# A WaveNet convolution kernel: a prologue with another load order, halo zeros set ahead, early staging copies on ScalarE and no filler matmuls

## The chip, the cores and the metric

The kernel runs on one core of one Trainium2 chip. The time is the device time of one execution in microseconds (us). Most executions of one kernel agree within about 0.3%. Before the change the median of the first three runs was 325.55 us (324.85 to 325.66).

## The reference

Sixteen thousand time steps of 144 channels in two batches go through a causal convolution of 15 taps at distance 2, a gate, and an output projection. All tensors are bf16.

```python
# x (2, 16000, 144), w (15, 144, 288), w_o (144, 144)
dil = 2
pad = (K - 1) * dil                       # 28 steps of halo
xp = jnp.pad(x, ((0, 0), (pad, 0), (0, 0)))
h = sum(einsum('btc,cd->btd', xp[:, pad - i*dil : pad - i*dil + T, :], w[i]) for i in range(K))
f, g = h[..., :D], h[..., D:]
z = jnp.tanh(f) * sigmoid(g)
return z @ w_o
```

## The kernel before

The 128 SBUF partitions hold 2 batches x 64 segments of 250 time steps. A partition also needs the 28 steps before its segment (its halo). For partitions 0 and 64, which start a batch, this halo is zero. The 144 channels are split into 128 ("A") and 16 ("B"). Names that the profile uses:

- `Xp` is the prologue's input (38 steps, loaded in four pieces), `Xr` the ring of later input chunks of 16 steps. `WA` are the 15 taps of the 128 channels, loaded in four pieces, youngest taps last. `WB` holds the weights of the 16 channels. `WOR` holds the output weights, 16 small loads on GpSimd's queue.
- `XA` and `XB` hold the input transposed. In the prologue TensorE transposes it (`ID,Xp`), and VectorE or ScalarE evacuates the bank (copies the result from `PS`, where TensorE writes, to SBUF). `UX` is a matmul result that ScalarE evacuates for a later addition on VectorE. Later input is copied to the staging buffers `STA` and `STB`, and a DMA transposes from there. `XBc` is a compacted copy of the 16 channels.
- The first ten steps are convolved directly (`WA,XA` and `WB,XB` matmuls). After them a fast scheme works on differences of inputs (`V`, `DU`, `DD`, `GU`, `GV`, `GX`, `GD`) and sums of weights (`WC`, `WS`, `WT`, `WV`, `WD`), both made on VectorE.

A small list scheduler in the kernel orders each engine's instructions at build time from estimated durations. An added or moved instruction can therefore reorder many others. The prologue's loads and fillers:

```python
wa_pieces = [(0, 4), (4, 8), (8, 12), (12, 15)]
pro_pieces = [(0, 14), (14, 22), (22, E0), (E0, EP)]
n16 = ((NP - 1) // 16) * 16                        # 112
for pi, (e0, e1) in enumerate(pro_pieces):
    if pi:
        ...  # g.add("sp", ld_w(t0, t1), ...): w3, w2, w1 ahead of x1, x2, x3
    if e0 >= H:
        ...  # last piece: all 128 partitions in one load
        continue
    g.add("sp", ld_x(flat(Xp[1:1 + n16, e0:e1, :]), 1, 1 + n16, e0, e1), ...)      # 112 partitions
    g.add("sp", ld_x(flat(Xp[1 + n16:NP, e0:e1, :]), 1 + n16, NP, e0, e1), ...)    # 15 partitions
...  # partition 0: two loads on ScalarE's queue
wa_op = g.add("sp", ld_w(t0, t1), w=[("WA", 0)], ...)       # w0, the youngest taps
...
warm(40)                                   # 40 matmuls that nobody reads, while the first load is under way
for pi in range(4):
    ...                                    # transposes, evacuation, compaction of piece pi
    warm(WARMS)                            # 8 filler matmuls
for o in range(-4, 0):
    ...                                    # VectorE memsets of the halo columns of XA
...                                        # GpSimd: zf, zf, fix: halo zeros of XBc
```

The staging copies, and what waits for the last weights:

```python
def load_xa(o):
    ...
    g.add("dve", lambda v: v.tensor_copy(STA[:, q, :, :], Xr[:, ci % NX, i0:i0 + 8, 0:DA]), ...)
    g.add("sp", lambda e: e.dma_start_transpose(XA[:, s, :, :], ...STA...), ...)
...
load_xchunk(0).deps.add(wa_op)             # input chunk 0 is issued when w0 has landed
...
op = g.add("pool", f, r=["WORz"], w=[("WORp", dl, part)], dma="wor", ...)   # output weights
op.deps.add(wa_op)
```

Of the kernel before, what the change touches and what calls it, by code (L numbers as in the profile page):

```python
# [327 lines left out]
def _conv_wavenet_kernel(nc, x, w, w_o, out):  # L328
# [39 lines left out]
    WARMS = 8  # L368
    LAG = 2
    PATTERNS = {29: 'O2 O1 Y01 Y0a D11 O0 Y0b D01 D00 D10', 28: 'Y0a X0a+ O1+ Y0b X0b+ O2+ D11 S0+ D10 X1a+ D00 Y01 S1+ X1b+ VE+ O0+ D01 VF+', 1: 'Y0a O2+ X0a+ Y0b X0b+ D11 X1a+ O1+ D00 S0+ D10 Y01 S1+ X1b+ D01 VE+ VF+ O0+', 0: 'Y0a X0a+ Y0b D11 X0b+ D00 X1a+ O2+ O1+ O0+ S0+ D10 Y01 S1+ X1b+ D01 VE+ VF+', 2: 'Y0a O2+ X0a+ O1+ Y0b X0b+ D11 D00 S0+ X1a+ D10 Y01 S1+ X1b+ D01 VE+ O0+ VF+'}  # L370
    SPREAD = 12
# [3 lines left out]
    with contextlib.ExitStack() as st:  # L375
# [111 lines left out]
        wa_pieces = [(0, 4), (4, 8), (8, 12), (12, 15)]  # L487
        pro_pieces = [(0, 14), (14, 22), (22, E0), (E0, EP)]
        n16 = ((NP - 1) // 16) * 16
        for pi, (e0, e1) in enumerate(pro_pieces):  # L490
            if pi:
                t0, t1 = wa_pieces[4 - pi]
                g.add("sp", ld_w(t0, t1), w=[("WA", 4 - pi)], dur=0.55, dma="wa", nbytes=(t1 - t0) * 128 * N2 * 2)
            if e0 >= H:
                g.add("sp", ld_x(flat(Xp[:, e0:e1, :]), 0, NP, e0, e1), w=[("Xp", pi, 0), ("Xp", pi, 1)], dur=0.45, dma="xp", nbytes=NP * (e1 - e0) * D * 2)
                continue
            g.add("sp", ld_x(flat(Xp[1:1 + n16, e0:e1, :]), 1, 1 + n16, e0, e1), w=[("Xp", pi, 0)], dur=0.45, dma="xp", nbytes=n16 * (e1 - e0) * D * 2)
            g.add("sp", ld_x(flat(Xp[1 + n16:NP, e0:e1, :]), 1 + n16, NP, e0, e1), w=[("Xp", pi, 1)], dur=0.45, dma="xp", nbytes=15 * (e1 - e0) * D * 2)
        g.add("act", lambda e: e.dma_start(flat(Xp[0:1, 0:H, :]), bass.AP(x_t, 0, [[L * D, 1], [1, H * D]])), w=[("Xp", 0, 2)], dur=0.5, dma="xp", nbytes=8064)
        g.add("act", lambda e: e.dma_start(flat(Xp[0:1, H:E0, :]), bass.AP(x_t, 0, [[L * D, 1], [1, KD * D]])), w=[("Xp", 2, 2)], dur=0.5, dma="xp", nbytes=576)  # L500
        t0, t1 = wa_pieces[0]
        wa_op = g.add("sp", ld_w(t0, t1), w=[("WA", 0)], dur=0.55, dma="wa", nbytes=(t1 - t0) * 128 * N2 * 2)
        xp_keys = [[("Xp", 0, 0), ("Xp", 0, 1), ("Xp", 0, 2)], [("Xp", 1, 0), ("Xp", 1, 1), ("Xp", 0, 2)],
                   [("Xp", 2, 0), ("Xp", 2, 1), ("Xp", 0, 2), ("Xp", 2, 2)], [("Xp", 3, 0)]]
# [11 lines left out]
        g.add("pool", lambda p: p.memset(Z[:], 0.0), w=[("Z", i) for i in range(NZ)], dur=1.2)  # L516
# [55 lines left out]
        for o in range(-4, 0):  # L572
            i0 = 2 if o == -4 else 0
            i1 = 6 if o == -1 else 8
            def zc(v, o_=o, i0_=i0, i1_=i1):
                dst = XA[:, aslot(o_), i0_:i1_, :].rearrange("p s (b q) -> p s b q", q=SEG)[:, :, :, 0]
                return v.memset(dst, 0.0)
            g.add("dve", zc, w=[("XA", aslot(o))], dur=0.08)
        hk = ["XBc_h%d" % i for i in range(4)]
        hk5 = hk + ["XBc_h4"]  # L580
        for b in range(B):
            def zf(p, b_=b):
                return p.memset(XBc[b_ * SEG:b_ * SEG + 1, 4:8, MB - H // 4 - 1:MB, :], 0.0)
            g.add("pool", zf, r=hk, w=hk + ["XBcz"], dur=0.35)


        def fix(p):
            s = Xp[:, H:E0, DA:D]
            dst = bass.AP(XBc[:].tensor, 6 * MB * DB + (MB - 1 - H // 4) * DB, [[8 * MB * DB, NP], [MB * DB, 2], [1, DB]])
            return p.tensor_copy(dst, s)  # L590
        g.add("pool", fix, r=xp_keys[2], w=hk, dur=0.3)
# [24 lines left out]
        def load_xchunk(ci):  # L616
            a, c = CH[ci]
            s = ci % NX
            return g.add("sp", ld_x(flat(Xr[:, s, 0:c - a, :]), 0, NP, E0 + a, E0 + c), w=[("Xr", s)], dur=0.5, dma="xr", nbytes=NP * (c - a) * D * 2)

        def compact_chunk(ci):
            a, c = CH[ci]
            s = ci % NX
            cmp_op("dve", Xr[:, s, 0:c - a, DA:D], E0 + a, E0 + c, [("Xr", s)], ("XBc", ci), 0.16 + (c - a) * DB / 1900.0)

        def diff_b(eng, m0, nm, r, tag):
# [5 lines left out]
            g.add(eng, f, r=r, w=[tag], dur=t_tt(4 * nm * DB), prio=2, soft=gate[:1])  # L632
# [5 lines left out]
        def load_xa(o):  # L638
# [3 lines left out]
            g.add("dve", lambda v: v.tensor_copy(STA[:, q, :, :], Xr[:, ci % NX, i0:i0 + 8, 0:DA]),  # L642
                  r=[("Xr", ci % NX)], w=[("STA", q)], dur=0.335, prio=2, soft=gate[:1])
# [3 lines left out]
        def load_xb(o, parts=(0, 1)):  # L647
# [10 lines left out]
            for h in parts:  # L658
                def cp(v, h=h):
                    src = bass.AP(XBc[:].tensor, (MB - 1 - m4 - h) * DB, [[8 * MB * DB, NP], [MB * DB, 6], [1, 128]])  # L660
                    return v.activation(STB[:, q, 6 * h:6 * h + 6, :], src, ACT.Copy)  # L661
                g.add("act", cp, r=sorted(ck, key=str), w=[("STB", q, h)], dur=0.708, prio=2, soft=gate[:1])
# [657 lines left out]
```

## Time and profile before

| | before |
|---|---|
| time, median of the first 3 runs | 325.55 us |
| span of the profiled run | 323.8 us |
| TensorE busy, 50 to 300 us | 249.98 of 250 us |
| first real work on TensorE | 5.62 us |
| first WB,XB / first WC,GX / first WA,GD / first projection | 21.53 / 31.09 / 40.87 / 46.82 us |

From the page of the kernel before, the head and the chain of work that ended last (shares of the span by engine):

```profile
span 323.8 us, 7023 instructions
...
PE 315.0 (97%) x2702; PEld 245.1 (76%) x2702; DVE 284.3 (88%) x616; ACT 265.3 (82%) x630; POOL 17.1 (5%) x29
...
## 4 chain that ended last, share of the span: by engine, by line
PE 89%; ACT 4%; DVE 3%; DMA 2%; issue 1%; POOL 0%; ACTq 0%; POOLq 0%
```

PE is TensorE's matmuls, PEld its weight loads. TensorE is the limit. VectorE (88%) is near, but has only 3% of the chain. Stretches of the same run, with columns: from and to, length, then busy time and instruction count of PE, PEld, DVE, ACT and POOL, then the granted clock, the share of time that the 16 DMA engines were busy, and GB/s. (The share sums the times of the packets, so it can pass 1: it is 1.35 from 20 to 25 us of this run.)

```profile
2.00:4.00 2.00, 2.00 (x21) 2.00 (x20) 0.00 (x0) 0.89 (x2) 2.00 (x1) 1.00 0.88 258
50.00:150.00 100.00, 99.98 (x841) 77.05 (x840) 94.31 (x201) 89.09 (x214) 0.00 (x0) 1.00 0.77 155
150.00:250.00 100.00, 100.00 (x846) 77.63 (x844) 94.18 (x200) 89.22 (x216) 0.00 (x0) 1.00 0.81 167
250.00:300.00 50.00, 50.00 (x422) 38.60 (x420) 41.40 (x85) 41.23 (x101) 0.00 (x0) 1.00 0.53 102
```

From 50 us on there is nothing to win by reordering: the sum of the last three PE columns is 249.98 us of 250. While the first inputs arrive, the DMA engines are 88% busy.

TensorE's weight-load timeline shows the prologue (start, duration, line, operands, how many; in brackets the idle time before it and what ended it):

```profile
5.62 0.82 PEld L559 LDWEIGHTS PS<-ID,Xp 128*128 128x128 bf16 x14
6.82 0.45 PEld L535 LDWEIGHTS PS<-ONES,ID 128*128 128x128 bf16 x8 [0.38 <-DVE XA L568]
...
21.53 1.45 PEld L729 LDWEIGHTS PS<-WB,XB 128*128 128x128 bf16 x12
...
26.42 0.11 PEld L729 LDWEIGHTS PS<-WT,DU 128*128 128x128 bf16 x2 [1.00 <-DVE DU L681]
...
30.79 0.24 PEld L729 LDWEIGHTS PS<-WA,XA 128*128 128x128 bf16 x3 [1.31 <-ACT UX L956]
...
40.87 0.11 PEld L729 LDWEIGHTS PS<-WA,GD 128*128 128x128 bf16 x2 [0.66 <-DVE PS L1020]
...
46.82 0.28 PEld L828 LDWEIGHTS PS<-WOR,ZT 128*128 128x128 bf16 x3
```

The second line is one of four filler groups (`ONES,ID`). The three large gaps sum to 2.97 us, and all begin after 25 us. The last line is the first projection. The chain of waits tells what they wait for (start, duration, what):

```profile
16.41 0.34 DVE STA L642
...
16.99 2.58 ACT STB L661 x4
19.56 6.65 DMA XB<-STB
...
26.24 1.58 ACT STB L661 x2
...
30.20 0.55 ACT UX L956
...
30.79 8.27 PE PS L729 x66
```

The staging copies for chunk 0 begin at 16.4 us, the first staged transpose takes 6.65 us from issue to landing, and ScalarE, held by its staging buffers, is late for the `UX` evacuation. That opens the gap of 1.31 us.

The load of chunk 0 was issued at 11.34 us, and the view of DMA issues (how many, KB, us from issue to landing) has for it:

```profile
Xr<-in_x_dram SPq DMA_DIRECT2D x1, 576.0 KB, 3.7
```

So it had landed at about 15.0 us, and VectorE, busy with weight sums, first read it at 16.20 us.

### The profile page before, as it was taken

Reading aid. Unit: us, or ns where it says so; the run is one execution under the profiler, and the core shown is the slowest. Engines: PE = TensorE matmul, PEld = TensorE weight load, DVE = VectorE, ACT = ScalarE, POOL = GpSimd, SP = SyncE. Lnnn points to the kernel's source line nnn. Section 1 sums busy time; section 2 is a strip of 40 time slices with the busy share of each in tenths; the row PEclk is TensorE's granted clock in tenths of the full one; section 3 lists DMA queues with packets and bytes.
Section 4 is the critical chain, followed back from the end, with each engine's and each line's share of the span. In section 5 each row is a group of like instructions: output and inputs, shape, how many; then the busy total and the mean of one; then the engine's idle time right before and its main releaser. Section 6 shows DMA issues by size and latency. Waiting matters only on the chain.

```text
span 323.8 us, 7023 instructions
## 1 busy us (share of the span) xinstructions
PE 315.0 (97%) x2702; PEld 245.1 (76%) x2702; DVE 284.3 (88%) x616; ACT 265.3 (82%) x630; POOL 17.1 (5%) x29
## 2 busy tenths in 40 slices
PE   7997999999999999999999999999999999999994
PEld 7875767777777777777777777777777777777774
DVE  1989979899898989989898998989899998884774
ACT  3666588979798998979898897989889797778674
POOL 8750000000000000000000000000000000000000
PEclk9999999999999999999999999999999999999999
DMA  8899992948849496897929888795958479161553
GB/s 210 277 119 224 188 236 63 183 134 159 220 92 222 102 201 169 126 238 106 249 69 218 154 167 189 90 225 122 224 141 175 102 115 197 37 75 75 109 125 97
DMA packets 127822, 50.40 MB, mean 156 GB/s; under 512 B 119134, under 2 KB 121615, under 8 KB 127789
## 3 DMA queue, kind: packets, MB, share of 16 engines
q1 hardware_dynamic: 127273, 49.62, 74.4%
q0 software_dynamic: 512, 0.33, 0.5%
q8 instruction: 21, 0.34, 0.4%
q14 instruction: 12, 0.10, 0.1%
q10 hardware_dynamic: 4, 0.01, 0.0%
HBM read 11.82 MB, written 9.22 MB: 65 GB/s over the span
## 4 chain that ended last, share of the span: by engine, by line
PE 89%; ACT 4%; DVE 3%; DMA 2%; issue 1%; POOL 0%; ACTq 0%; POOLq 0%
PE PS L729 77%; PE PS L828 9%; DMA XB<-STB 2%; ACT STB L661 2%; PE PS L535 1%; DVE WC L610 1%; ACT TS L750 1%; ACT TS L753 0%; ACT PS L887 0%; DVE V L681 0%; DVE WT L610 0%; DVE WD L610 0%; ACT XA L568 0%; PE PS L859 0%; PE PS L786 0%
## 5 line engine op out<-in xcount | busy, mean ns | idle before, releaser
L1008 DVE TENSOR_TENSOR Xp<-PS,UX 128x576 f32<-128x576 f32 x90 | 62.8, 750 | 20.4 <-PE PS L729 20.1
L729 PE MATMUL PS<-WB,XB 128*128 128x288 bf16 x260 | 71.9, 286 | 0.0
L729 PE MATMUL PS<-WA,GD 128*128 128x288 bf16 x360 | 69.9, 286 | 0.4 <-DVE PS L1020 0.4
L1020 DVE TENSOR_TENSOR PS<-PS,Xp 128x576 f32<-128x576 f32 x90 | 68.2, 758 | 2.1 <-ACT OS L836 1.0
L750 ACT ACTIVATE TS<-PS 128x288 f16<-128x288 f32 x125 | 51.6, 413 | 15.0 <-PE PS L729 14.0
L836 ACT ACTIVATE OS<-PS 128x432 bf16<-128x432 f32 (+1 forms) x88 | 42.3, 488 | 13.8 <-PE PS L828 12.8
L661 ACT ACTIVATE STB<-XBc 128x768 bf16<-128x768 bf16 x60 | 50.5, 849 | 3.4 <-DMA XB<-STB 2.0
L753 ACT ACTIVATE TS<-PS 128x288 f16<-128x288 f32 x125 | 51.4, 411 | 0.0
L887 ACT ACTIVATE PS<-PS 128x288 f32<-128x288 f32 x120 | 46.1, 405 | 4.2 <-PE PS L729 4.1
L956 ACT ACTIVATE UX<-PS 128x576 f32<-128x576 f32 x60 | 39.2, 654 | 10.4 <-PE PS L729 10.1
L729 PE MATMUL PS<-WS,GU 128*128 128x288 bf16 x210 | 44.3, 287 | 0.0
L828 PE MATMUL PS<-WOR,ZT 128*128 128x144 bf16 (+1 forms) x322 | 42.4, 253 | 0.0
L729 PEld LDWEIGHTS PS<-WA,GD 128*128 128x128 bf16 x360 | 34.6, 98 | 10.0 <-DVE PS L1020 1.2
L758 DVE TENSOR_TENSOR Z<-TS 128x288 bf16<-128x288 f16 x125 | 36.7, 298 | 4.5 <-ACT TS L753 4.2
L729 PE MATMUL PS<-WC,XB 128*128 128x288 bf16 x120 | 34.3, 286 | 0.0
L828 PEld LDWEIGHTS PS<-WOR,ZT 128*128 128x128 bf16 x322 | 27.9, 98 | 6.3 <-ACT OS L836 0.5
L729 PE MATMUL PS<-WD,DD 128*128 128x288 bf16 x180 | 31.9, 286 | 0.5 <-ACT PS L887 0.5
L729 PE MATMUL PS<-WC,V 128*128 128x288 bf16 x180 | 30.6, 286 | 0.0
L729 PE MATMUL PS<-WA,DD 128*128 128x288 bf16 x180 | 30.6, 286 | 0.0
L729 PEld LDWEIGHTS PS<-WB,XB 128*128 128x128 bf16 x260 | 25.4, 98 | 6.4
L729 PE MATMUL PS<-WT,DU 128*128 128x288 bf16 x120 | 24.5, 286 | 0.8 <-DVE DU L681 0.7
L729 PEld LDWEIGHTS PS<-WS,GU 128*128 128x128 bf16 x210 | 18.5, 98 | 7.5 <-ACT PS L887 0.3
(80 smaller groups left out, 468.7 us busy)
## 6 DMA issues: line engine op xcount, KB each, us to landing
Xr<-in_x_dram SPq DMA_DIRECT2D x15, 576.0 KB, 4.5
out_dram<-OS SPq DMA_DIRECT2D x30, 288.0 KB, 3.2
WA<-in_w_dram SPq DMA_DIRECT2D x3, 288.0 KB, 5.0
ZT<-Z SPq DMA_TRANSPOSE x32, 3.7
Xp<-in_x_dram SPq DMA_DIRECT2D x2, 252.0 KB, 4.8
XA<-STA SPq DMA_TRANSPOSE x30, 3.5
XB<-STB SPq DMA_TRANSPOSE x30, 4.8
Xp<-in_x_dram SPq DMA_DIRECT2D x1, 441.0 KB, 3.9
```

What stands on the lines that cost most here:

```text
L535: g.add("pe", [lambda t: t.matmul(PS[:, BANK_O * 512:BANK_O * 512 + 128], lhsT=ID[:], rhs=ONES[:], start=True, stop=True)] * n, r=["ID", " ...
L661: return v.activation(STB[:, q, 6 * h:6 * h + 6, :], src, ACT.Copy)
L729: return lambda t: t.matmul(bank(bk.b), lhsT=lhs(), rhs=rhs(), start=start, stop=True, skip_group_check=True)
L750: return a.activation(TS[:, s, 0, :, :], both(bk, 0, D), ACT.Tanh)
L753: return a.activation(TS[:, s, 1, :, :], both(bk, D, D), ACT.Sigmoid)
L758: return v.tensor_tensor(dst, TS[:, s, 0, :, :], TS[:, s, 1, :, :], ALU.mult)
L828: return t.matmul(PS[:, c0:c0 + n * D], lhsT=ZT[:, zt, blk, :], rhs=WOR[:, wi:wi + n, :].rearrange("p a b -> p (a b)"), start=first, stop= ...
L836: return e.tensor_copy(dst, src) if eng == "dve" else e.activation(dst, src, ACT.Copy)
L887: g.add("act", lambda e: e.activation(bank(bk.b + 1), bank(bk.b), ACT.Copy), w=[bk], dur=t_act(N2), prio=0)
L956: g.add("act", lambda e: e.activation(UX[:, k, u % NU, :, :], both(X, 0, N2), ACT.Copy), r=[X], w=[("UX", k, u % NU)], frees=[X], dur=t_ac ...
L1008: g.add("dve", lambda v, k=k, wi=wi, vb=vb, us=us: v.tensor_tensor(wslot(wi), both(vb, 0, N2), UX[:, k, us, :, :], ALU.add), r=[vb, ("UX", ...
L1020: return v.tensor_tensor(both(d, 0, N2), src, wslot(wi), ALU.add)
```

## The change

The intent is to have the staged transposes begin earlier: chunk 0 is loaded ahead of the youngest weights, its staging copies go to ScalarE, the halo zeros are written before any data lands, later loads keep out of the first transposes' way, and TensorE no longer runs fillers. The core of the diff:

```diff
-    WARMS = 8
+    WARMS = 0
...
+    EARLY = 4
+    EARLYC = 1
...
+        LOADS = [("x", 0), ("w", 3), ("w", 2), ("x", 1), ("w", 1), ("x", 2), ("x", 3), ("r", 0), ("w", 0)]
...
-            g.add("sp", ld_x(flat(Xp[1:1 + n16, e0:e1, :]), 1, 1 + n16, e0, e1), ...)
-            g.add("sp", ld_x(flat(Xp[1 + n16:NP, e0:e1, :]), 1 + n16, NP, e0, e1), ...)
+            for i, p0 in enumerate((0, SEG)):
+                g.add("sp", ld_x(flat(Xp[p0 + 1:p0 + SEG, e0:e1, :]), p0 + 1, p0 + SEG, e0, e1), ...)   # 63 partitions
...
+        for zi, (e0, e1) in enumerate(((0, 14), (14, H))):
+            for p0 in (0, SEG):
+                g.add("dve", lambda v, ...: v.memset(flat(Xp[p0:p0 + 1, e0:e1, :]), 0.0), ...)
...
-            g.add("dve", zc, w=[("XA", aslot(o))], dur=0.08)
...  (GpSimd's zf, zf and fix are gone too)
-            cmp_op("dve", Xr[:, s, 0:c - a, DA:D], ...)
+            cmp_op("act" if ci <= EARLYC else "dve", Xr[:, s, 0:c - a, DA:D], ...)
...
+            if o <= EARLY:
+                g.add("act", lambda a: a.activation(STA[:, q, :, :], src, ACT.Copy), ...)
+            else:
+                g.add("dve", lambda v: v.tensor_copy(STA[:, q, :, :], src), ...)
...
-        load_xchunk(0).deps.add(wa_op)
+        if ("r", 0) not in LOADS:
+            load_xchunk(0).deps.add(wa_op)
...
-                op.deps.add(wa_op)            # output weights
+                op.deps.add(xb2)              # xb2: the second staged transpose
...
-                load_xchunk(nl[0]).deps.add(wa_op)
+                load_xchunk(nl[0]).deps.add(wa_op if nl[0] < 2 else xb2)
```

The full diff also changes what the scheduler may do (priorities, work held back until the second staged transpose, the bank of one accumulator, finer tracking of `Z`).

More of the change, by code (lines that the diff above doesn't have):

```diff
@@ L487, in _conv_wavenet_kernel, with load_xchunk @@
         wa_pieces = [(0, 4), (4, 8), (8, 12), (12, 15)]
+        LOADS = [("x", 0), ("w", 3), ("w", 2), ("x", 1), ("w", 1), ("x", 2), ("x", 3), ("r", 0), ("w", 0)]
         pro_pieces = [(0, 14), (14, 22), (22, E0), (E0, EP)]
-        n16 = ((NP - 1) // 16) * 16
-        for pi, (e0, e1) in enumerate(pro_pieces):
-            if pi:
-                t0, t1 = wa_pieces[4 - pi]
-                g.add("sp", ld_w(t0, t1), w=[("WA", 4 - pi)], dur=0.55, dma="wa", nbytes=(t1 - t0) * 128 * N2 * 2)
+        def load_xchunk(ci):
+            a, c = CH[ci]
+            s = ci % NX
+            return g.add("sp", ld_x(flat(Xr[:, s, 0:c - a, :]), 0, NP, E0 + a, E0 + c), w=[("Xr", s)], dur=0.5, dma="xr", nbytes=NP * (c - a) * D * 2)
@@ L494, in _conv_wavenet_kernel @@
+        wa_ops = {}
+        for what, pi in LOADS:
+            if what == "w":
+                t0, t1 = wa_pieces[pi]
+                wa_ops[pi] = g.add("sp", ld_w(t0, t1), w=[("WA", pi)], dur=0.42, dma="wa", nbytes=(t1 - t0) * 128 * N2 * 2)
+                continue
+            if what == "r":
+                load_xchunk(pi)
+                continue
+            e0, e1 = pro_pieces[pi]
             if e0 >= H:
-                g.add("sp", ld_x(flat(Xp[:, e0:e1, :]), 0, NP, e0, e1), w=[("Xp", pi, 0), ("Xp", pi, 1)], dur=0.45, dma="xp", nbytes=NP * (e1 - e0) * D * 2)
+                g.add("sp", ld_x(flat(Xp[:, e0:e1, :]), 0, NP, e0, e1), w=[("Xp", pi, 0), ("Xp", pi, 1)], dur=0.48, dma="xp", nbytes=NP * (e1 - e0) * D * 2)
@@ L496, in _conv_wavenet_kernel @@
                 continue
-            g.add("sp", ld_x(flat(Xp[1:1 + n16, e0:e1, :]), 1, 1 + n16, e0, e1), w=[("Xp", pi, 0)], dur=0.45, dma="xp", nbytes=n16 * (e1 - e0) * D * 2)
-            g.add("sp", ld_x(flat(Xp[1 + n16:NP, e0:e1, :]), 1 + n16, NP, e0, e1), w=[("Xp", pi, 1)], dur=0.45, dma="xp", nbytes=15 * (e1 - e0) * D * 2)
-        g.add("act", lambda e: e.dma_start(flat(Xp[0:1, 0:H, :]), bass.AP(x_t, 0, [[L * D, 1], [1, H * D]])), w=[("Xp", 0, 2)], dur=0.5, dma="xp", nbytes=8064)
-        g.add("act", lambda e: e.dma_start(flat(Xp[0:1, H:E0, :]), bass.AP(x_t, 0, [[L * D, 1], [1, KD * D]])), w=[("Xp", 2, 2)], dur=0.5, dma="xp", nbytes=576)
@@ L501, in _conv_wavenet_kernel @@
-        t0, t1 = wa_pieces[0]
-        wa_op = g.add("sp", ld_w(t0, t1), w=[("WA", 0)], dur=0.55, dma="wa", nbytes=(t1 - t0) * 128 * N2 * 2)
-        xp_keys = [[("Xp", 0, 0), ("Xp", 0, 1), ("Xp", 0, 2)], [("Xp", 1, 0), ("Xp", 1, 1), ("Xp", 0, 2)],
-                   [("Xp", 2, 0), ("Xp", 2, 1), ("Xp", 0, 2), ("Xp", 2, 2)], [("Xp", 3, 0)]]
+            for i, p0 in enumerate((0, SEG)):
+                g.add("sp", ld_x(flat(Xp[p0 + 1:p0 + SEG, e0:e1, :]), p0 + 1, p0 + SEG, e0, e1), w=[("Xp", pi, i)], dur=0.48, dma="xp", nbytes=63 * (e1 - e0) * D * 2)
@@ new lines, in _conv_wavenet_kernel @@
+        for p0 in (0, SEG):
+            g.add("act", ld_x(flat(Xp[p0:p0 + 1, H:E0, :]), p0, p0 + 1, H, E0), w=[("Xp", 2, 2 + p0)], dur=0.5, dma="xp", nbytes=576)
+        for zi, (e0, e1) in enumerate(((0, 14), (14, H))):
+            for p0 in (0, SEG):
+                g.add("dve", lambda v, p0=p0, e0=e0, e1=e1: v.memset(flat(Xp[p0:p0 + 1, e0:e1, :]), 0.0), w=[("XpZ", zi, p0)], dur=1.1)
+        xpz = [[("XpZ", zi, p0) for p0 in (0, SEG)] for zi in range(2)]
+        xp_keys = [[("Xp", 0, 0), ("Xp", 0, 1)] + xpz[0], [("Xp", 1, 0), ("Xp", 1, 1)] + xpz[1],
+                   [("Xp", 2, 0), ("Xp", 2, 1), ("Xp", 2, 2), ("Xp", 2, 2 + SEG)] + xpz[1], [("Xp", 3, 0), ("Xp", 3, 1)]]
@@ L506, in ld_wb @@
+        wa_op = wa_ops[0]
         def ld_wb(par):
@@ L515, in _conv_wavenet_kernel @@
         g.add("pool", lambda p: p.memset(XBc[:, 4:6, MB - 1, :], 0.0), w=["XBcz"], dur=0.2)
-        g.add("pool", lambda p: p.memset(Z[:], 0.0), w=[("Z", i) for i in range(NZ)], dur=1.2)
+        g.add("pool", lambda p: p.memset(Z[:], 0.0), w=[("Z", i, d) for i in range(NZ) for d in range(8)], dur=1.2)
         g.add("pool", lambda p: p.memset(WOR[:], 0.0), w=["WORz"], dur=1.9)
@@ L571, in _conv_wavenet_kernel @@
             warm(WARMS)
-        for o in range(-4, 0):
-            i0 = 2 if o == -4 else 0
-            i1 = 6 if o == -1 else 8
-            def zc(v, o_=o, i0_=i0, i1_=i1):
-                dst = XA[:, aslot(o_), i0_:i1_, :].rearrange("p s (b q) -> p s b q", q=SEG)[:, :, :, 0]
-                return v.memset(dst, 0.0)
-            g.add("dve", zc, w=[("XA", aslot(o))], dur=0.08)
         hk = ["XBc_h%d" % i for i in range(4)]
         hk5 = hk + ["XBc_h4"]
-        for b in range(B):
-            def zf(p, b_=b):
-                return p.memset(XBc[b_ * SEG:b_ * SEG + 1, 4:8, MB - H // 4 - 1:MB, :], 0.0)
-            g.add("pool", zf, r=hk, w=hk + ["XBcz"], dur=0.35)
-        def fix(p):
-            s = Xp[:, H:E0, DA:D]
-            dst = bass.AP(XBc[:].tensor, 6 * MB * DB + (MB - 1 - H // 4) * DB, [[8 * MB * DB, NP], [MB * DB, 2], [1, DB]])
-            return p.tensor_copy(dst, s)
-        g.add("pool", fix, r=xp_keys[2], w=hk, dur=0.3)
         for o, tiles, bb in ((-1, range(E0 - 4, E0), 7), (0, range(E0, E0 + 8), 6)):
@@ L614, in chunk_of @@
             return [ci for ci, (a, c) in enumerate(CH) if a <= t < c][0]
-        def load_xchunk(ci):
-            a, c = CH[ci]
-            s = ci % NX
-            return g.add("sp", ld_x(flat(Xr[:, s, 0:c - a, :]), 0, NP, E0 + a, E0 + c), w=[("Xr", s)], dur=0.5, dma="xr", nbytes=NP * (c - a) * D * 2)
         def compact_chunk(ci):
@@ L623, in compact_chunk @@
             s = ci % NX
-            cmp_op("dve", Xr[:, s, 0:c - a, DA:D], E0 + a, E0 + c, [("Xr", s)], ("XBc", ci), 0.16 + (c - a) * DB / 1900.0)
+            cmp_op("act" if ci <= EARLYC else "dve", Xr[:, s, 0:c - a, DA:D], E0 + a, E0 + c, [("Xr", s)], ("XBc", ci), 0.16 + (c - a) * DB / 1900.0)
         def diff_b(eng, m0, nm, r, tag):
@@ L631, in f @@
                 return v.tensor_tensor(pat(2, -2 * MB * DB), pat(6, -2 * MB * DB), pat(4, 2 * MB * DB + DB), ALU.subtract)
-            g.add(eng, f, r=r, w=[tag], dur=t_tt(4 * nm * DB), prio=2, soft=gate[:1])
+            g.add(eng, f, r=r, w=[tag], dur=t_tt(4 * nm * DB), prio=2 if gate else 0, soft=gate[:1])
         def diff_chunk(ci):
@@ L641, in load_xa @@
             i0 = 8 * o - CH[ci][0]
-            g.add("dve", lambda v: v.tensor_copy(STA[:, q, :, :], Xr[:, ci % NX, i0:i0 + 8, 0:DA]),
-                  r=[("Xr", ci % NX)], w=[("STA", q)], dur=0.335, prio=2, soft=gate[:1])
+            src = Xr[:, ci % NX, i0:i0 + 8, 0:DA]
+            if o <= EARLY:
+                g.add("act", lambda a: a.activation(STA[:, q, :, :], src, ACT.Copy), r=[("Xr", ci % NX)], w=[("STA", q)], dur=0.92, prio=1, soft=gate[:1])
+            else:
+                g.add("dve", lambda v: v.tensor_copy(STA[:, q, :, :], src), r=[("Xr", ci % NX)], w=[("STA", q)], dur=0.335, prio=2, soft=gate[:1])
             g.add("sp", lambda e: e.dma_start_transpose(XA[:, s, :, :], STA[:, q, :, :].rearrange("p a b -> p (a b)")),
@@ L661, in cp @@
                     return v.activation(STB[:, q, 6 * h:6 * h + 6, :], src, ACT.Copy)
-                g.add("act", cp, r=sorted(ck, key=str), w=[("STB", q, h)], dur=0.708, prio=2, soft=gate[:1])
+                g.add("act", cp, r=sorted(ck, key=str), w=[("STB", q, h)], dur=0.708, prio=2 if gate else 0, soft=gate[:1])
             if 1 not in parts:
                 return
-            g.add("sp", lambda e: e.dma_start_transpose(XB[:, s, :, :], STB[:, q, :, :].rearrange("p a b -> p (a b)")),
+            return g.add("sp", lambda e: e.dma_start_transpose(XB[:, s, :, :], STB[:, q, :, :].rearrange("p a b -> p (a b)")),
                   r=[("STB", q, 0), ("STB", q, 1)], w=[("XB", s)], dur=1.7, dma="xb", nbytes=12 * 128 * 128 * 2)
@@ L811, in ship @@
             g.add("sp", lambda e: e.dma_start_transpose(ZT[:, zt, d0:9, :], Z[:, z, d0 * 128:9 * 128]), r=[("Z", z, d) for d in dls],
-                  w=[("ZT", zt)], dur=1.3, dma="zt", nbytes=(9 - d0) * 32768)
+                  w=[("ZT", zt)], dur=1.3, dma="zt", nbytes=(9 - d0) * 32768, soft=(xb2,))
         GROUPS = ((0, 3), (3, 6), (6, 8))
@@ L1062, in direct_b @@
                   r=[("XB", bslot(-1)), ("XB", bslot(0)), ("WB", 0), ("WB", 1)], w=[b.bk], floating=k >= KF, prio=2 if k >= KF else 1, dur=2 * MM)
-        load_xchunk(0).deps.add(wa_op)
-        dp = [_Bank(2 * i % 8, 2) for i in range(5)]
+        if ("r", 0) not in LOADS:
+            load_xchunk(0).deps.add(wa_op)
+        dp = [_Bank(2 * i if i < 4 else None, 2) for i in range(5)]
         db = [_Half(dp[k // 2], k % 2) for k in range(10)]
@@ L1100, in _conv_wavenet_kernel @@
         load_xa(2)
-        load_xb(2)
+        xb2 = load_xb(2)
         for i in range(4):
@@ L1184, in _conv_wavenet_kernel @@
         done_d = {}
+        gate[:] = [xb2]
         for f in stage(1):
             f()
+        gate[:] = []
         for f in prepare(0):
```

## The prediction

> **What bounds it now.** From about 44 us TensorE runs without a break: the stretches from 50 to 300 us show it 249.98 of 250 us busy, and the chain of waits is 86% matmul lines. Both kernels' instruction orders differ only in the first 317 of 2,673 TensorE instructions and then run alike, so the change can only shift the steady part. What can be won lies before 44 us. In the timeline TensorE starts real work at 5.62 us, when its 40 warm-up matmuls end (the first input chunk had landed at 5.07). After that I count weight-load gaps of 0.38, 1.00, 1.31, 0.66 and 0.31 us, and four groups of 8 filler matmuls at 0.40 to 0.52 us: 3.7 us of gaps, 1.9 us of fillers. About 5.5 us (1.7%) is the ceiling.
>
> **Why those gaps.** The chain of waits goes over VectorE's weight sums (to 16.3 us), ScalarE's staging copies (16.99 to 19.56), the first staged transpose (6.65 us to landing, 26.24) and ScalarE until 30.8.
>
> **What the change does.**
> - 32 fillers go, 1.9 us of TensorE time; partly they only filled waits.
> - Input chunk 0 is loaded ahead of the youngest weights. Before, it was issued at 11.34 us, after they had landed, and used at 16.2.
> - VectorE loses five staging copies of 0.41 us, two compactions of 0.21, four memsets of 0.07. ScalarE gains five of about 1.0 us (its 1,024-column copy takes 1.02) and two of 0.35.
> - GpSimd's halo zeroing (1.09 + 0.29 us) leaves the path. Four VectorE memsets come before data lands, free.
> - Output-weight loads and input chunk 2 wait for the second staged transpose.
> - A hidden cost: input loads were 112+15 partitions and become 63+63. The Trainium skill ("DMA: Bandwidth & Descriptors", section "Why a DMA increments its semaphore by 16 and not by 1") says a transfer uses the largest number of engines up to 16 that divides the partitions: 63 gives nine, the lowest-numbered. This trace doesn't show engines. A 4,032-byte packet took 156 ns, a 2,304-byte one 108: nine engines then carry 14 rows instead of 8, worth 0.9 + 0.65 + 0.65 us of delay. I estimate chunk 0 landing near 13.7 us, the last weights near 15.
>
> **On the critical path.** Laid out in the new order with the trace's durations: ScalarE takes chunk 0 at 13.7, two staging copies, one evacuation and a compaction to 17, four staging copies to 20, then the XB evacuation to 21.5. TensorE reaches the WB,XB matmuls near 21 and waits; before, it ran them at 21.53. So far nearly nothing is gained. But TensorE has 12 matmuls more done when it reaches the first WC,GX (before 31.09, now about 30.7); the UX gap of 1.31 us shrinks, and the first WA,GD group (40.87) comes 1 to 1.5 us earlier. If 63 rows do spread evenly, the gain is about 2.4 us.
>
> **Prediction: 323.9 us** (-0.5%), range 322.3 to 325.3 at 8 in 10. Faster by over 2%: 0.01; within 2%: 0.98; slower: 0.01.
>
> **What would show it.** First transposes at 5.6 to 6.0 us; chunk 0's compaction on ScalarE at 13 to 14.5; WB,XB matmuls at 20.3 to 21.7, held by ScalarE's XB evacuation; less idle at UX; the steady part identical, shifted by 1 to 2 us; no drop in granted clock without fillers; output weights landed before the first projection near 45.5.
>
> **What would make it wrong.** If nine-engine loads are false, 323 or less. If ScalarE's heavier queue holds bank evacuations longer than I reckon, or the delayed output weights and chunk 2 collide with later transposes, the gain vanishes. If the second staged transpose lands much earlier, more gaps close: 322.

## The result, and the profile after

Ratios in this document are the mean time of one kernel's fast runs over the mean of the other's from the same rounds, so they are not quite the ratio of the medians that are quoted.

| | before | after |
|---|---|---|
| median, 6 runs each in the same rounds | 325.49 us (324.52 to 326.07) | 324.33 us (323.99 to 325.67) |
| ratio, 95% interval | | 0.9975 (0.9951 to 0.9998) |
| span of the profiled run | 323.8 us | 322.6 us |
| granted clock of the profiled run | 0.998 | 1.000 |
| first WB,XB | 21.53 | 22.45 |
| first WC,GX | 31.09 | 31.47 |
| first WA,GD | 40.87 | 39.60 |
| first projection | 46.82 | 45.49 |

The change brought 1.2 us of median, which is "the same" at two per cent. The first projection is 1.33 us earlier, the span 1.2 us shorter. Everything happened in the prologue. Stretches of the kernel after, columns as before:

```profile
2.00:4.00 2.00, 2.00 (x22) 2.00 (x21) 1.48 (x3) 0.84 (x2) 2.00 (x1) 1.00 0.51 169
50.00:150.00 100.00, 99.98 (x843) 77.09 (x841) 94.26 (x202) 89.31 (x215) 0.00 (x0) 1.00 0.76 157
150.00:250.00 100.00, 100.00 (x844) 77.49 (x842) 93.64 (x199) 89.22 (x215) 0.00 (x0) 1.00 0.84 169
250.00:300.00 50.00, 50.00 (x424) 38.69 (x422) 41.94 (x84) 40.39 (x101) 0.00 (x0) 1.00 0.43 97
```

The steady part is as busy as before. The clock stayed at 1.00 without fillers. But in the first line the DMA share fell from 0.88 to 0.51 and the rate from 258 to 169 GB/s, although as many loads wait to be served. Weight-load timeline of the kernel after:

```profile
6.33 0.78 PEld L575 LDWEIGHTS PS<-ID,Xp 128*128 128x128 bf16 x14 [0.63 <-DMA Xp<-in_x_dram]
...
10.04 0.45 PEld L575 LDWEIGHTS PS<-ID,Xp 128*128 128x128 bf16 x8 [0.67 <-DMA Xp<-in_x_dram]
...
12.80 0.46 PEld L575 LDWEIGHTS PS<-ID,Xp 128*128 128x128 bf16 x8 [1.10 <-issue]
...
22.45 1.34 PEld L725 LDWEIGHTS PS<-WB,XB 128*128 128x128 bf16 x12 [0.36 <-ACT XB L598]
...
31.47 0.36 PEld L725 LDWEIGHTS PS<-WC,GX 128*128 128x128 bf16 x4 [0.21 <-ACT PS L883]
...
39.60 0.11 PEld L725 LDWEIGHTS PS<-WA,GD 128*128 128x128 bf16 x2 [0.35 <-DVE PS L1016]
...
45.49 0.28 PEld L824 LDWEIGHTS PS<-WOR,ZT 128*128 128x128 bf16 x3
```

The late gaps have shrunk: the gaps over 0.2 us between WB,XB and the first projection sum to 3.28 us before (1.00, 1.31, 0.66, 0.31) and 1.12 us after (0.21, 0.32, 0.35, 0.24). In their place the early part has new ones: up to WB,XB they sum to 3.45 us, against 0.38 before. In 2.40 us of this (0.63, 0.67, and 1.10 by the reading below) TensorE waits for input, in the rest for evacuations. "<-issue" at 12.80 means that the profile shows no cause. The third piece of input is the likely one, as ScalarE's compaction of the same piece waited for that load until 12.77 us. The chain of waits after:

```profile
5.86 8.97 DMA Xr<-in_x_dram
...
14.85 1.06 ACT STA L637
15.91 0.91 ACT XA L584
16.82 0.30 ACT XBc L544
17.12 0.95 ACT STA L637
18.07 2.93 ACT STB L657 x4
21.00 1.40 ACT XB L598 x2
```

Chunk 0 was issued at 5.86 us instead of 11.34, but took 8.97 us to land. The staging copy starts at 14.85 instead of 16.34, so 5.5 us of earlier issue became 1.5 us. Even this is mostly not the load's: chunk 0 landed at 14.83 us, against about 15.0 before, so the earlier issue brought the landing forward by 0.2 us only. By the two traces the rest comes from the copy's move to ScalarE, which took the chunk up at once, where VectorE had left it for 1.2 us. ScalarE then works through its list to the `XB` evacuation at 22.4 us, for which TensorE waits.

### The profile page after: what moved, and what is told of

It reads as the page before. It is cut to its first block, busy times and chain, and to the rows that moved or that the text cites. A ratio compares the mean times of both kernels' runs of the same rounds, so it can differ in the third digit from the quotient of the medians.

```text
span 322.6 us, 6961 instructions
## 1 busy us (share of the span) xinstructions
PE 314.0 (97%) x2670; PEld 243.0 (75%) x2670; DVE 285.8 (89%) x610; ACT 269.4 (83%) x636; POOL 15.4 (5%) x26
## 4 chain that ended last, share of the span: by engine, by line
PE 86%; DVE 4%; ACT 4%; DMA 3%; SPq 1%; issue 1%; ACTq 0%
PE PS L725 76%; PE PS L824 9%; DMA Xr<-in_x_dram 3%; SPq L475 1%; ACT STA L637 1%; ACT STB L657 1%; DVE V L677 1%; DVE Xp L1004 1%; DVE DD L677 1%; ACT XB L598 0%; DVE DU L677 0%; SPq L487 0%; PE PS L855 0%; DVE Z L754 0%; PE PS L782 0%
## 5 line engine op out<-in xcount | busy, mean ns | idle before, releaser
L1004 DVE TENSOR_TENSOR Xp<-PS,UX 128x576 f32<-128x576 f32 x90 | 62.8, 750 | 19.6 <-PE PS L725 19.3
L677 DVE TENSOR_TENSOR V<-XA 128x1024 bf16<-128x1024 bf16 (+2 forms) x39 | 23.5, 607 | 0.9 <-ACT XA L584 0.9
```

Source lines behind the costliest of these rows:

```text
L677: return g.add("dve", lambda v: v.tensor_tensor(dst, a, b, ALU.subtract), r=r, w=wk, dur=t_tt(n), prio=prio, soft=gate[:1])
L1004: g.add("dve", lambda v, k=k, wi=wi, vb=vb, us=us: v.tensor_tensor(wslot(wi), both(vb, 0, N2), UX[:, k, us, :, :], ALU.add), r=[vb, ("UX", ...
```

## The experiments

Twelve kernels were run, all with five rounds beside the kernel before; all gave a correct result. The median of the kernel before was 325.49, 325.44 and 325.53 us in the three calls. The third call ran on another chip than the first two; where its kernels are compared with earlier ones, their ratios to the kernel before are the safer measure. The landmark times come from each kernel's own profile, one execution each, and they scatter: in even_rows, even_outw_early, even_pool and even_fillers, which issue chunk 0 at the same time (8.3 us) behind the same loads, it was copied at 12.88 to 13.96 us. In 13 of the 14 profiles the span is 277.0 to 277.5 us longer than the start of the first projection, so the spans tell roughly when it began in the runs without a profile.

| kernel | median us (range) | ratio (95%) | chunk 0 copied | WB,XB | projection |
|---|---|---|---|---|---|
| before | 325.49 | 1 | 16.34 | 21.53 | 46.82 |
| after | 324.33 (323.99 to 325.67) | 0.9975 (0.9951 to 0.9998) | 14.85 | 22.45 | 45.49 |
| even_rows | 323.22 (322.80 to 324.49) | 0.9943 (0.9922 to 0.9964) | 13.20 | 20.79 | 43.82 |
| before_rows63 | 328.06 (327.37 to 328.67) | 1.0081 (1.0061 to 1.0101) | 19.29 | 24.55 | 49.68 |
| before_nofill | 324.82 (324.22 to 326.46) | 0.9992 (0.9969 to 1.0014) | 16.20 | 20.70 | 45.33 |
| after_fillers | 324.69 (324.16 to 324.90) | 0.9979 (0.9963 to 0.9995) | 14.50 | 22.63 | 45.42 |
| even_chunk0_last | 323.89 (323.40 to 324.43) | 0.9951 (0.9935 to 0.9966) | 14.77 | 22.37 | 45.40 |
| even_outw_early | 324.37 (323.46 to 326.08) | 0.9982 (0.9959 to 1.0005) | 12.94 | 20.54 | 44.64 |
| even_dve_copies | 324.41 (324.08 to 326.50) | 0.9981 (0.9958 to 1.0004) | 14.43 | 20.96 | 45.85 |
| even_actq | 324.68 (324.23 to 326.53) | 0.9985 (0.9962 to 1.0008) | 13.99 | 21.71 | 47.71 |
| even_fillers | 323.62 (323.47 to 323.70) | 0.9946 (0.9933 to 0.9958) | 13.96 | 21.64 | 44.79 |
| even_actq2 | 321.99 (321.91 to 322.58) | 0.9901 (0.9885 to 0.9918) | 12.47 | 20.07 | 43.11 |
| even_pool | 323.89 (323.57 to 324.31) | 0.9955 (0.9942 to 0.9967) | 12.88 | 21.74 | 44.77 |
| even_pool_actq | 324.21 (323.87 to 324.65) | 0.9964 (0.9951 to 0.9977) | 12.88 | 22.12 | 45.17 |

The theory going in was that of the prediction: the change is worth some 2.4 us, and the 63-partition loads take back about half, since they run on nine DMA engines. The rivals were that the loads are as fast as before and something else holds the chain (the order of loads, ScalarE's longer queue, the deferred output weights), and that the missing fillers cost or bring time by themselves, by the clock or by TensorE time.

### Rows in parts that divide evenly, in the kernel after

```diff
-   g.add("sp", ld_x(... p0 + 1, p0 + SEG ...), ...)                                        # 63 partitions
+   g.add("sp", [ld_x(... q0, q1 ...) for q0, q1 in ((p0 + 1, p0 + 49), (p0 + 49, p0 + SEG))], ...)   # 48 and 15
-   slot[1] += 16
+   slot[1] += 16 * len(op.fns)      # each of the two loads adds 16 to the semaphore
```

All compute orders are unchanged.

> The changed kernel with each 63-row input load split into 48+15 rows inside the same place of the queue; the order of every compute engine is unchanged. Theory (63 rows run on nine of sixteen DMA engines): first transposes at about 5.7 us instead of 6.33, second input piece landed near 8 instead of 10.03, chunk 0 on ScalarE at 12.5 to 13 instead of 14.85, WB,XB matmuls near 20.5 to 21 instead of 22.45, whole kernel 1 to 2 us faster than the changed kernel (322.3 to 323.3). Rival (the new order of the loads alone delays the input): landings stay within 0.3 us and the time within 0.3 us of the changed kernel's 324.33.

Measured: 323.22 us, ratio 0.9943; first projection 43.82, which is 1.67 us earlier than in the kernel after. The same stretch of its windows:

```profile
2.00:4.00 2.00, 2.00 (x22) 2.00 (x20) 1.48 (x3) 0.84 (x2) 2.00 (x1) 1.00 0.76 202
```

From its weight-load timeline and its chain of waits:

```profile
5.91 0.79 PEld L575 LDWEIGHTS PS<-ID,Xp 128*128 128x128 bf16 x14 [0.20 <-DMA Xp<-in_x_dram]
...
43.82 0.28 PEld L824 LDWEIGHTS PS<-WOR,ZT 128*128 128x128 bf16 x3
```

```profile
8.30 4.87 DMA Xr<-in_x_dram
```

The DMA share is back at 0.76, and chunk 0 lands after 4.87 us instead of 8.97. The four landmarks that wait for input move by 0.42 us (first transposes, 6.33 to 5.91), 1.06 (second piece, 10.04 to 8.98), 1.63 (third, 12.80 to 11.17) and 1.65 (chunk 0, 14.85 to 13.20). The gaps ahead of WB,XB sum to 1.64 us instead of 3.45. The time and WB,XB came as the theory expected, the landings 0.2 to 1.0 us later than it expected. The row cut is a real cost of the change, on the critical path. Its profiled run was the slowest of its six (324.49 us), and there the last output store took about 5.0 us instead of 3.1 or less, so its span says less than its landmarks. The spans of its other five runs (321.0 to 322.4 us), less 277, put their first projection at 44.0 to 45.4 us. This is an estimate, but by it the profiled prologue was the quickest of the six, and differences from 43.82 are some 0.3 us too large.

### The same row cut in the kernel before

```diff
-   ld_x(... 1, 113 ...)      # 112 partitions
-   ld_x(... 113, 128 ...)    # 15
+   ld_x(... 1, 64 ...)                               # 63
+   ld_x(... 65, 128 ...), ld_x(... 64, 65 ...)       # 63 and 1
```

> The kernel before with only its input rows cut 63+63+1 instead of 112+15; nothing else changed. Theory (nine engines): first transposes at 6.3 us instead of 5.62, last weights landed about 2 us later, first staging copy from chunk 0 at 18 instead of 16.34, whole kernel 1 to 2 us slower (326.5 to 327.5). Rival: no change beyond 0.3 us.

```profile
2.00:4.00 2.00, 2.00 (x21) 2.00 (x20) 0.00 (x0) 0.86 (x2) 2.00 (x1) 1.00 0.57 171
```

Measured: 328.06 us, 2.6 us slower (ratio 1.0081), first projection 2.86 us later. The DMA share is 0.57; nine of sixteen engines would be 0.56. The direction was right and the size larger than expected: here chunk 0 is only issued when the last weights have landed (15.04 instead of 11.34 us). Of these 3.70 us, 2.95 arrive at the staging copy (16.34 to 19.29) and 2.86 at the first projection. The single-partition load adds to it; its part was not separated.

The Trainium skill ("DMA: Bandwidth & Descriptors", section "Why a DMA increments its semaphore by 16 and not by 1") says that a transfer uses the largest number of engines, up to 16, that divides the slowest dimension on both of its sides, which for these loads is the partitions. The trace carries no engine numbers, and the share (0.51 and 0.57 with 63 rows, 0.88 and 0.76 with 112 and 48) is only a sum of packet times. But the packet log that is kept with each trace has the start and duration of every packet, and shows how many were in flight at once. From 2.0 to 3.5 us the first piece (packets of 4,032 bytes) had 9.0 in flight on average in the kernel after and 8.5 in before_rows63, against 14.9 in the kernel before and 12.1 in even_rows. The median packet took 156 to 159 ns in all four. So the 63-row loads had fewer packets in flight, not slower ones, and their number agrees with nine engines.

### Fillers taken from the kernel before, and given to the kernel after

```diff
-   [matmul] * n
+   [matmul] * (n if n > 8 else 0)      # before_nofill: the 32 fillers out, orders kept
+   [matmul] * (n or 8)                 # after_fillers: 32 fillers in, orders kept
```

> The kernel before without its four groups of 8 filler matmuls, all orders otherwise unchanged. Theory (in the kernel before the fillers cover waits; the gaps further on are ended by VectorE, ScalarE and the transposes): 0 to 0.3 us faster, WT,DU matmuls still at 26.4 and the wait for UX still until 30.8. Rival (the removed fillers are the gain): 1.0 to 1.9 us faster. Second rival (fillers hold the TensorE clock up): slower, with a granted clock below 1 in the first 15 us.

> The changed kernel with the four groups of 8 filler matmuls put back, all orders otherwise unchanged. Theory: two groups fall into waits for input, two cost up to 0.5 us each, and ScalarE's XB evacuation hides part of that: 0.1 to 0.7 us slower. Rival (fillers are the whole gain): 1.2 us slower or more, back to the kernel before.

Measured: before_nofill has a ratio of 0.9992 (0.9969 to 1.0014), so its gain lies between -0.5 and 1.0 us: not settled. Its profile shows the projection 1.49 us earlier, but in that execution the first staged transpose also landed after 5.1 us instead of 6.65, so the landmark doesn't settle it either. WT,DU came at 25.09 us and the wait for `UX` ended at 29.30, where 26.4 and 30.8 were expected: a miss. Its clock was 1.00. In after_fillers, where TensorE waits for input in the same places, the projection came at 45.42 against 45.49: the fillers ran inside waits and cost nothing that shows there. The ratios (0.9979 and 0.9975) differ by 0.1 us and the medians by 0.4, within the spread, so the cost of 0.1 to 0.7 us that was expected is neither seen nor excluded. Removing fillers brought nothing measurable to the kernel after as it stands. Nor did the clock need them: the Trainium skill ("TensorE: Matmul & The Clock Gate", section "What's actually happening") gives an idle window of about 3.4 us before the clock falls; the longest gap in the kernel after, once TensorE has begun, is 1.10 us, and the clock stayed at 1.00.

### The remaining parts, one at a time, on the base of even_rows

With the load cost out of the way, each part of the change was taken back alone.

```diff
# even_chunk0_last: after scheduling, chunk 0's load and w0's change places
+   sp[i], sp[j] = wa_op, r0
# even_outw_early: the output weights wait for w0 again, as before the change
+   op.deps.discard(xb2); op.deps.add(wa_op)
# even_dve_copies: copies and compactions back on VectorE (rescheduled)
-   EARLY = 4; EARLYC = 1
+   EARLY = 0; EARLYC = -1
# even_fillers: 32 fillers in, orders kept
+   [matmul] * (n or 8)
```

> As even_rows, but input chunk 0 is queued behind the youngest weights instead of ahead of them; all compute orders unchanged. Theory (chunk 0 sets off ScalarE's staging, which holds the WB,XB matmuls): chunk 0 reaches ScalarE about 1 to 1.5 us later than 13.2, WB,XB matmuls at 21.8 to 22.3 instead of 20.8, first projection about 1 us later than 43.8, time 0.5 to 1.5 us above even_rows (323.7 to 324.7). Rival (the order of these two does not matter, the weights bind VectorE just as much): within 0.3 us of even_rows.

> As even_rows, but the sixteen output-weight loads wait only for the youngest weights, as in the kernel before, not for the second staged transpose; all orders unchanged. Theory (the deferral buys little, since ScalarE is busy with other work when the staged transposes land): the two transposes of STB land up to 1.5 us later, time within 0.4 us of even_rows (322.8 to 323.6). Rival (the contention is what made the kernel before slow at 26 us): a wait for the transposes reappears on ScalarE and the time is 1 us or more above even_rows.

> As even_rows, but the staging copies and compactions of the first chunks are on VectorE again, with the order worked out anew. Theory (ScalarE's chain of copies ahead of the XB evacuation binds at WB,XB, but VectorE is as full): WB,XB matmuls earlier than 20.8 by 0.5 to 1.5 us, but the later WT,DU and WC,GX matmuls wait for VectorE again; time 0 to 1 us above even_rows. Rival (moving the copies to ScalarE was a loss): faster than even_rows by over 0.5 us.

> As even_rows, with the four groups of 8 filler matmuls put back; all orders unchanged. Theory (whether fillers cost anything depends on whether TensorE would wait there anyway; even_rows waits only about 1.6 us before WB,XB against 3.4 in the changed kernel, where the fillers cost nothing at the first projection): first projection 0.3 to 1.0 us later than 43.8, time 0.2 to 1.0 us above even_rows. Rival (fillers never cost anything here): no shift of the first projection beyond 0.1 us.

Measured, in delay of the first projection against even_rows (43.82): 1.58 us for chunk 0 behind w0, 0.82 for early output weights, 2.03 for copies on VectorE, 0.97 for fillers. The first three sum to 4.43 us, while all parts together bring 3.00 (46.82 to 43.82); in medians the three are 0.67, 1.15 and 1.19 us, and all together 2.27. So they seem not to be additive, as if each removed partly the same wait. This is not shown: each ratio's interval is 0.5 to 0.75 us each way. The 0.97 is not the fillers' alone, as said below. The zeroing of the halo was not separated, nor the gate on chunk 2.

The expectation for the order of loads hit in the landmarks, which moved even slightly more than it said. In time the medians differ by 0.67 us, but the ratios (0.9951 and 0.9943) only by 0.3, so the time does not exclude the rival. That for the output weights missed: at most 0.4 us was expected. The rival (1 us or more, with a wait for the transposes on ScalarE) came true: 1.15 us in medians. ScalarE's timeline of even_outw_early, then TensorE's weight loads of the same run, show how it comes:

```profile
25.16 1.58 ACT L657 ACTIVATE STB<-XBc 128x768 bf16<-128x768 bf16 x2 [0.34 <-DMA XB<-STB]
...
27.55 0.84 ACT L657 ACTIVATE STB<-XBc 128x768 bf16<-128x768 bf16 x1 [0.52 <-DMA XB<-STB]
```

```profile
27.63 0.13 PEld L725 LDWEIGHTS PS<-WS,GU 128*128 128x128 bf16 x2 [0.98 <-ACT PS L883]
```

The first two staged transposes of `XB` landed 7.5 and 6.5 us after issue, against 4.5 and 5.5 in even_rows (4.5 and 5.6 in the kernel after): 3.0 and 1.0 us longer with the output weights loading beside them. ScalarE waited for its staging buffers, and a gap of 0.98 us opened on TensorE; even_rows and the kernel after have neither. Deferring the output weights is therefore a part that works: it keeps small loads out of the transposes' way. In time the intervals of the two kernels just touch (0.9959 and 0.9964); the profiled run was the fastest of its six.

With copies on VectorE, WB,XB was not earlier (20.96, where 19.3 to 20.3 was expected, against 20.79), and the later matmuls waited on VectorE for 0.69 (WT,DU at 35.83) and 1.29 us (WA,DD at 37.72), since the differences come later. With fillers on this base TensorE reaches WB,XB at 21.64, 0.85 us later. But in this execution chunk 0, issued at the same 8.30 us, took 5.6 us to land instead of 4.9, and ScalarE waited for it:

```profile
13.96 1.06 ACT L637 ACTIVATE STA<-Xr 128x1024 bf16<-128x1024 bf16 x1 [0.64 <-DMA Xr<-in_x_dram]
```

ScalarE then began the `XB` evacuation 0.77 us later (20.02 against 19.25), so WB,XB would have been late without fillers too. Whether fillers cost anything on this base stays open; the times show no difference (0.9946 to 0.9943).

### Issue time: loads on a second queue

```diff
# even_actq: second halves of x0 and x1 issued from ScalarE's queue (rescheduled)
-   g.add("sp", [ld_x(...)...
+   g.add("act" if i and pi < 2 else "sp", [ld_x(...)...
-   "xp": 8
+   "xp": 10            # semaphores for prologue loads
# even_actq2: only the second half of x0, moved after scheduling; all orders kept; "xp": 10
+   first = [op for op in g.order["sp"] if op.dma == "xp"][1]
+   move(first, "act", 0)
```

> A try at a better kernel: as even_rows, with the second half of the first two input pieces issued from ScalarE's queue, and enough semaphores that the fourth piece waits for none; order worked out anew. Expected: first transposes at 5.7 instead of 5.91 (issue of the loads is shared by two queues), chunk 0 on ScalarE 0.5 to 1 us earlier than 13.2, time 322.4 to 323.2, so 0 to 0.8 us below even_rows. If the DMA engines and not the issue bind here, no change.

> As even_rows, with only the second half of the first input piece issued from ScalarE's queue and enough semaphores that the fourth piece waits for none; this time all compute orders are kept (even_actq lost them). Expected: chunk 0 on ScalarE 0.3 to 1 us earlier than 13.2, WB,XB matmuls at 20.2 to 20.6, first projection 0 to 0.6 us earlier than 43.8, time 0 to 0.6 us below even_rows. If it is no better than even_rows, then even_actq did not lose through its order alone.

Measured: even_actq missed, at 324.68 us. The scheduler gave another order, in which TensorE waits 1.52 us at WA,GD (in a profiled run that was the slowest of the six); the edit tested a new schedule more than a second queue. even_actq2, with the orders kept, took 321.99 us, ratio 0.9901, the fastest kernel. The first input loads on SyncE's queue, first of even_rows, then of even_actq2 (both loads of the other half now go out on ScalarE's queue), and the windows of even_actq2:

```profile
0.81 1.81 SPq L475 DMA_DIRECT2D Xp<-in_x_dram  x4
```

```profile
0.80 0.91 SPq L475 DMA_DIRECT2D Xp<-in_x_dram  x2
```

```profile
2.00:4.00 2.00, 2.00 (x22) 2.00 (x21) 1.48 (x3) 1.51 (x2) 2.00 (x1) 1.00 0.93 261
```

Each issue took SyncE about 0.45 us here, so four of them hold up what follows by 1.8 us. Halving that brings the DMA share to 0.93, chunk 0's issue from 8.30 to 7.68 us, its copy from 13.20 to 12.47, and the projection from 43.82 to 43.11. The last evacuation moved by the same 0.71 us. The medians differ by 1.2 us. The profile of even_rows explains part of the half microsecond beyond 0.71, as it was some 0.3 us ahead of the other runs by the estimate above; the rest is open, and the runs were on two chips. On the same chip as even_actq2, even_pool with the loads of even_rows had chunk 0 at 12.88, only 0.41 us later. The ratios (0.9943 and 0.9901, intervals of about 0.002 each way) give a gain of 1.4 us, give or take 0.9, if the two intervals are independent. The two edits, queue and semaphores, were not separated by a run. But in even_rows the issue of the fourth piece took 0.38 us, no longer than the others, so there was no wait that more semaphores could end (in the kernel after it took 1.13 us); the queue is the likely cause. The expected gain was 0 to 0.6 us, so this was a miss upward.

### Staging copies on GpSimd

```diff
# even_pool: the first two STA copies move from ScalarE's list to GpSimd's, ahead of the output weights
+   for op in [op for op in g.order["act"] if op in sta_ops[:2]]:
+       move(op, "pool", ...)
# even_pool_actq: this and even_actq2's edits together
```

> As even_rows, with the first two staging copies on the idle GpSimd instead of ScalarE; all other orders kept. Expected if ScalarE's copies are what holds WB,XB (theory): GpSimd takes 1 to 1.5 us for a copy, the wait of 0.33 us at WB,XB goes, first projection 0.2 to 0.8 us earlier. What could spoil it: GpSimd slows VectorE while both work, or its copies take over 2 us and the staged transposes come later; then slower than even_rows.

> Both of the last two edits together. Expected: about the sum of the two shifts, first projection at 42.8 to 43.6, time 322.0 to 323.2; the best of all kernels if both work.

Both missed: 323.89 and 324.21 us, slower than without the move (0.9955 against 0.9943, 0.9964 against 0.9901). For the first pair the time intervals overlap, but the landmarks agree: the projection came 0.95 us later. The first of the two fears, that GpSimd slows VectorE, came true. GpSimd's and VectorE's timelines of even_pool:

```profile
12.88 2.30 POOL L639 COPY STA<-Xr 128x1024 bf16<-128x1024 bf16 x2 [5.37 <-DMA Xr<-in_x_dram]
```

```profile
13.05 1.22 DVE L624 TENSOR_TENSOR XBc<-XBc 128x448 bf16<-128x448 bf16 x1
14.20 1.25 DVE L679 TENSOR_TENSOR DU<-XA 128x512 bf16<-128x512 bf16 x1
```

The same two VectorE instructions in even_rows:

```profile
13.51 0.38 DVE L624 TENSOR_TENSOR XBc<-XBc 128x448 bf16<-128x448 bf16 x1
13.81 0.42 DVE L677 TENSOR_TENSOR DU<-XA 128x512 bf16<-128x512 bf16 x1
```

While GpSimd copied, the two subtractions on VectorE took three times as long, and each ended about when a GpSimd copy of 1.15 us ended (14.27 and 15.45 against about 14.0 and 15.18). ScalarE then waited for VectorE and reached the XB evacuation later: WB,XB at 21.74 after a gap of 1.74 us. The Trainium skill ("SBUF — State Buffer", section "Who interferes with whom") says that a VectorE instruction with two SBUF inputs contends with a GpSimd instruction that reads SBUF, and calls the contention for the shared ports an exclusive lock. This trace agrees, with 0.38 to 1.22 and 0.42 to 1.25 us.

## Why the prediction was right, and where it was off

The total was right: 323.9 predicted, 324.33 measured, in the range of 322.3 to 325.3. Point by point:

- **"The change can only shift the steady part."** Right. TensorE was busy 249.98 us of 250 after as well, and the shift at the first projection (1.33 us) is nearly the difference of the medians (1.16 us).
- **The loads of 63 partitions use nine engines.** Right, by the packets in flight, and both row experiments and the DMA share agree. The term of 0.9 + 0.65 + 0.65 = 2.2 us of delay for chunk 0 measured 1.65 us against even_rows, which however pays two more issues for each piece. Against even_actq2, which has most of the first piece's issue time out of the way, it is 2.38 us (14.85 to 12.47). The size was good, within a scatter of about a microsecond in chunk 0's landing.
- **"If 63 rows do spread evenly, the gain is about 2.4 us."** Right in medians: even_rows gained 2.27 us (325.49 to 323.22). By the first projection it gained 3.00.
- **First transposes at 5.6 to 6.0 us.** Too early: 6.33. The first input had landed at 5.07 us before; with the 0.9 us reckoned for the row cut that is 5.97. It landed at 6.31, so this term was 0.3 us short.
- **Chunk 0's copy at 13.7, WB,XB at 20.3 to 21.7.** Too early by about 1.1 us: 14.85 and 22.45. The step named, "laid out in the new order with the trace's durations", started from an estimate of chunk 0's landing that was 1.1 us short, and this went through the list. The delay by the row cut, 2.2 us of it, was sized well, so it was the base under it that was short: 11.5 us with even rows (13.7 less 2.2), where the best that was measured is 12.47 (even_actq2). The durations of ScalarE's list held: from the first copy to WB,XB the prediction needed at most 8.0 us (13.7 to 21.7), and the run took 7.6 (14.85 to 22.45). The chunk's compaction came at 16.72 instead of 13 to 14.5, as one staging copy and one evacuation go first.
- **WB,XB held by ScalarE's XB evacuation.** Right, with an idle time of 0.36 us named by the trace.
- **"12 matmuls more done" at the first WC,GX, and the UX gap shrinks.** Right in kind. WC,GX came at 31.47 (30.7 predicted), later than before, but with those matmuls done, and the gap of 1.31 us is gone. WA,GD came 1.27 us earlier, in the predicted 1 to 1.5. This is partly luck: the run was 0.77 us behind the prediction at WC,GX and on time at WA,GD, and no step of the prediction says where these 0.77 us would be made good.
- **"Input chunk 0 is loaded ahead of the youngest weights."** In this change it gave almost nothing by itself: the landing moved from about 15.0 to 14.83 us, as the row cut took the rest, and the copy gained mainly by its move to ScalarE. With even rows chunk 0 landed at 13.17.
- **Fillers: "partly they only filled waits".** Right for the kernel after, where putting them back moved the projection by -0.07 us. What they cost the kernel before stays open.
- **Output weights landed in time.** Right: issued from 28.2 to 36.2 us, landed within 6.5 us, before the first projection at 45.49. That deferring them is itself worth 0.8 us at the first projection on an even load was not seen.

The total came out 0.43 us above the prediction. Chunk 0's late landing is the mis-sized term that points that way, but no run isolates it, and 0.43 us is within the spread of the runs. What stays open: the worth of the fillers in the kernel before, of the halo zeros, of the gate on chunk 2, of the scheduling hints, of the fillers on even rows, and of even_actq2's two edits each.

## What to carry to other kernels

When a load is cut into row groups, choose counts that divide evenly over the DMA engines: two loads of 63 rows cost more than four loads of 48, 15, 48 and 15, and the sign of it is a low DMA share in a stretch where loads are queued, and few packets in flight. When a load is moved forward, compare its landing, and not only its issue or its first use. When TensorE is saturated later, read a prologue change from landmarks (when the first matmul of each kind starts) and from the gaps between them. Take several profiles of each kernel: the landing of chunk 0 moved by a microsecond here between kernels with the same loads, which made fillers look costly. When testing one part of a change in a kernel with a build-time scheduler, keep the orders and edit after scheduling; otherwise the experiment measures another schedule.

## What the Trainium skill lacked or had wrong

- "DMA: Bandwidth & Descriptors", section "Why a DMA increments its semaphore by 16 and not by 1", gives the rule for the number of engines but neither what it costs nor how a profile shows it. Here the trace has no engine numbers; the busy share of the DMA engines from 2 to 4 us shows it (0.51 and 0.57 with 63 rows, 0.88 with 112 and 15), and so do the packets in flight (9.0 and 8.5 against 14.9); the cost was 2.6 us of 325 in before_rows63, with one single-row load more a piece.
- The same page, section "Issuing engines are not separate DMA queues", says that issuing from several engines saves only sequencer time, "which is usually small relative to the DMA itself". At the start of this kernel it was not small: about 0.45 us an issue, 1.81 us for four, and moving two of them to a second queue (with two more semaphores) brought chunk 0's issue 0.62 us and the first projection 0.71 us forward.
- The same page, section "Latency and other measured facts", gives a bandwidth for the DMA transpose (261 GB/s on one kernel), but no time under contention. A staged transpose of 393,216 bytes (12 tiles of 128x128 bf16) took 4.5 and 5.5 us from issue to landing in even_rows, and 7.5 and 6.5 us with the output weights loading beside it. At 6.5 us that is 60 GB/s, with latency and queueing in it.
- "SBUF — State Buffer" was right on the contention of VectorE and GpSimd, and "TensorE: Matmul & The Clock Gate" on short gaps that leave the clock alone (1.10 us, clock 1.00).
